# Queries and keys in one load, probabilities read back in four, output sums stored in one

## The chip, the cores and the metric

The kernel runs on one core of a Trainium2 chip. The metric is device time in microseconds, the median of several runs, as the host starts the program once and waits for its end. The core has five engines that run side by side: TensorE (PE, with its weight loads shown apart as PEld), VectorE (DVE), ScalarE (ACT), GpSimd (POOL) and SyncE (SP), which does no arithmetic and here issues nearly all DMA transfers. Each engine takes its instructions in order, and an instruction that has to wait for another engine or for a transfer holds up those behind it.

## The reference

Attention within chunks of 64 tokens, 8 batches of 8 heads, 576 tokens, 64 channels to a head; its rows, put together over the heads, go through a normalized, gated pair of layers:

```
scores = scale * q_c @ k_c.T          # per chunk of 64 tokens
attn   = softmax(scores)              # over the chunk
x      = (attn @ v_c)                 # 4608 rows of 8 * 64 = 512
xn     = x / sqrt(mean(x * x) + 1e-6) * rms_g
g, val = xn @ w_gate, xn @ w_val      # 512 -> 1536
out    = (g * sigmoid(g) * val) @ w_out   # 1536 -> 512
```

Everything is float32. The kernel splits each operand of the large products into a high and a low part and sums three matmuls.

## The kernel before

The attention is done in 18 units of 256 tokens (`UT`), each in two halves of 128 tokens, `i = 2 * u` and `2 * u + 1`. The layers are done in tiles of 512 tokens: three plain ones first (`t` = 0, 1, 2, the loop over `PLAIN`), then three pairs of tiles, in which the products are done by a Strassen-like scheme of seven products for eight on sums of blocks (`P1` to `P7`, the names of the products).

A unit goes through a list of steps, `unit_steps`, which are hung on the loop of the layers at numbered places (`PAIR_AT` and `PAIR_STEPS` and their like), so that its work lies between the large matmuls: `load_unit` loads queries and keys (L233, L234); `first` makes the scores on PE (L264) and the exponentials; `load_values` loads values (L240); `second` sums them and turns blocks of 32x32 on DVE (L355); `away` stores the probabilities of both halves to DRAM (L360, `away_e`); `third`, `turn_back`, reads them back in another arrangement (L371, tile `eT`); `fourth` multiplies them with the values (L388) and normalizes (L402 to L410, tile `xu`). In `mean_square` (L455) the tile `eT` serves as a place for squares nobody reads. Then `xu` is turned on DVE, stored (L421) and read back as `x` (L428). Units 0 to 3 use another way with transposes on PE (`att_transpose`, L321 to L323), which also writes a tile with the tag `eT`.

Before a tile can be written, the readers of what stood in its buffer must be done. The pool `io` has four buffers of 4 KB to a partition; queries `qt`, keys `kt`, values `vt`, `xu` and, during tile `t` = 1, the sums `w` of output weights take turns in them. The pool `att` has two buffers for `eT`.

Each unit's queries and keys are two transfers of 512 KB. The probabilities of a unit are read back in eight transfers of 64 KB, by half `s`, by `c` and by `k`, into two tiles, one for each `c`. The sums of output weights are made in `out_sides` in three steps: `sums` (L614 and L623 on DVE), `parts` (L627 on ACT, L628 on DVE), `store` (L633). There are 12 of them, four in tile `t` = 1 and eight in `t` = 2 (there in `spots` of the second `x` or in a tile of their own). Each is stored to the DRAM tensor `wol` in two transfers of two slots each. Beside them, in `t` = 1, `sides` loads converted weights back (L664), sums them on POOL (L659), splits them on ACT and DVE (L687, L689) and stores them (L688, L690). In the pairs the weights are read from DRAM by `ring_load` (L743, `wr`) and `out_load` (L859, L863, `wo`).

The order of the work: up to the end of `t` = 0 a planner that knows the durations of instructions only from a model orders all engines by priority; from `t` = 1 on PE keeps the order in which the program is written, and in the pairs SP, DVE and ACT keep it too. In `t` = 1 and 2 the planner still orders SP, DVE and ACT. By the profile `t` = 1 runs from about 150 to 254 us, `t` = 2 from there to 366, and the three pairs from there on.

Of the kernel before, what the change touches and what calls it, by code (L numbers as in the profile page):

```python
# [8 lines left out]
F32 = mybir.dt.float32  # L9
# [8 lines left out]
P = 128  # L18
CH = 64
D = 64  # L20
H = 8
NPAIR = H // 2
N = 4608
UT = 256
# [27 lines left out]
Q = 32  # L52
# [38 lines left out]
def tile_chunk_attn_swiglu(  # L91
    ctx: ExitStack,
    tc: tile.TileContext,
    qT: bass.AP,
    kT: bass.AP,
    v: bass.AP,
    w_up: bass.AP,
    w_out: bass.AP,
# [3 lines left out]
    nc = tc.nc  # L102
# [1 line left out]
    const = ctx.enter_context(tc.tile_pool(name="const", bufs=1))  # L104
    xs = ctx.enter_context(tc.tile_pool(name="xs", bufs=2 * NDT))
    dram = ctx.enter_context(tc.tile_pool(name="dram", bufs=1, space=bass.MemoryType.DRAM))
    io = ctx.enter_context(tc.tile_pool(name="io", bufs=4))
    wts = ctx.enter_context(tc.tile_pool(name="wts", bufs=3 * NF // 2))
    att = ctx.enter_context(tc.tile_pool(name="att", bufs=2))
    small = ctx.enter_context(tc.tile_pool(name="small", bufs=4))  # L110
# [28 lines left out]
    def bank(pool, name):  # L139
        return pool.tile([P, 512], F32, tag=pool_tag[id(pool)], name=name)  # L140
# [87 lines left out]
    state = {}  # L228

    def load_unit(u):  # L230
        qt = io.tile([P, NPAIR, UT], F32, tag="io", name="qt")
        kt = io.tile([P, NPAIR, UT], F32, tag="io", name="kt")
        nc.sync.dma_start(qt, qT[u])  # L233
        nc.sync.dma_start(kt, kT[u])  # L234
        for s in range(2):
            state[2 * u + s] = {"q": qt, "k": kt}

    def load_values(u):
        vt = io.tile([P, NPAIR, UT // CH, D], F32, tag="io", name="vt")
# [4 lines left out]
    def load_first_unit():  # L244

        qt, kt = (x[:, 2 * i : 2 * i + 2].rearrange("p s (a t) -> p (s a) t", t=UT) for i in range(2))
        for s in range(2):
            part = slice(s * P, (s + 1) * P)
            nc.sync.dma_start(qt[:, :, part], qT[0][:, :, part])
            nc.scalar.dma_start(kt[:, :, part], kT[0][:, :, part])  # L250
            state[s] = {"q": qt, "k": kt}

    def two_banks(pool, name):
# [62 lines left out]
    def att_transpose(i, pool=None):  # L316
        st = state[i]
        e = st["e"].rearrange("p a j k -> p a (j k)")
        eT = st["eT"] = att.tile([P, NPAIR, P], F32, tag="eT", name="eT")
        pt = bank(pool or ps_a, "ps_t").rearrange("p (a k) -> p a k", k=P)  # L320
        for pr in range(NPAIR):  # L321
            nc.tensor.transpose(pt[:, pr], e[:, pr], ident)
        nc.scalar.copy(eT, pt)  # L323
# [38 lines left out]
    def turn_back(i):  # L362
        st, s = state[i], i % 2
        if s == 0:
            state["eT", i // 2] = [att.tile([P, 2, H, Q], F32, tag="eT", name="eT") for _ in range(2)]
        eT, away = state["eT", i // 2], st["away"]
        back = away.rearrange("(c t p) (k r) -> c k p t r", c=2, t=2, k=2)
        for c in range(2):
            for k in range(2):
                dst = slice((2 * s + k) * Q, (2 * s + k + 1) * Q)  # L370
                nc.sync.dma_start(eT[c][dst].rearrange("p t h q -> p t (h q)"), back[c, k])  # L371

    def turned_values(u):
        subs = [state[2 * u + s] for s in range(2)]
        for st in subs:
            st["o"] = bank(ps_a, "ps_o")
        vt = subs[0]["v"].rearrange("p a n d -> p (a n d)").rearrange("p (c h d) -> p c h d", c=2, d=D)
        eT = state.pop(("eT", u))  # L380
        for s, st in enumerate(subs):
            st["eT"] = eT[s]
        for h in range(H):
            for t in range(2):
                for c in range(2):
                    for s, st in enumerate(subs):
                        rows = slice(s * CH, (s + 1) * CH)
                        nc.tensor.matmul(  # L388
                            st["o"][(2 * c + t) * Q : (2 * c + t + 1) * Q, h * D : (h + 1) * D],
                            eT[c][rows, t, h],  # L390
                            vt[rows, c, h],
                            start=True,
                            stop=True,
                        )
# [205 lines left out]
    def out_sides(i, c, home):  # L600

        cols = slice(c * P, (c + 1) * P)
        hi, lo = (
            out_parts[i][:, n].bitcast(F32).rearrange("p f (h c) -> p (f h) c", c=KH)[:, :, cols]
            for n in range(2)
        )
        slots = wol_.rearrange("p (k i) c -> p i k c", i=NPR)[:, i, :, c * KH : (c + 1) * KH]

        ws = []

        def sums():
            ws.append(home())
            w = ws[0]
            nc.vector.tensor_tensor(w[:, :, 0], hi, lo, op=ALU.add)  # L614
            a11, a21, a12, a22 = (w[:, n, 0] for n in range(4))
            s1, s2, s4, s3 = (w[:, n, 1] for n in range(4))
            for o, one, two, op in (
                (s1, a21, a22, ALU.add),
                (s2, s1, a11, ALU.subtract),
                (s4, a12, s2, ALU.subtract),  # L620
                (s3, a11, a21, ALU.subtract),
            ):
                nc.vector.tensor_tensor(o, one, two, op=op)  # L623

        def parts():
            w = ws[0]
            nc.scalar.copy(w[:, :, 0].bitcast(F32R), w[:, :, 1])  # L627
            nc.vector.tensor_tensor(w[:, :, 1].bitcast(F32R), w[:, :, 1], w[:, :, 0], op=ALU.subtract)  # L628

        def store():  # L630
            w = ws[0]
            for n in range(0, 4, 2):
                nc.sync.dma_start(slots[:, n : n + 2], w[:, n : n + 2].rearrange("p n a c -> p n (a c)"))  # L633

        return [sums, parts, store]

# [344 lines left out]
    def unit_steps(u, x):  # L981
# [19 lines left out]
        def third():  # L1001
            for i in both:
                turn_back(i)

        def fourth():
            turned_values(u)
            turned_norm(u)

        return [
            lambda: load_unit(u),  # L1010
            first,
            lambda: load_values(u),
# [9 lines left out]
    class Steps:  # L1022
# [4 lines left out]
        def __call__(self):  # L1027
            for f in self.at.get(self.n, ()):
                f()
            self.n += 1  # L1030

    load_first_unit()
    conv_load(0)
    load_values(0)
    load_unit(1)
    load_values(1)
    nc.sync.dma_start(g_col, rms_g)
# [5 lines left out]
    softmax(0)  # L1043
    softmax(1)
    att_transpose(0)
    softmax_sum(0)
    att_transpose(1)
    o = two_banks(ps_h, "ps_o")
    att_values(0, o)
# [6 lines left out]
    scores(3, s2)  # L1056
    softmax(3)
    att_transpose(2)
    softmax_sum(2)
    x_transpose_unit(0)  # L1060
# [11 lines left out]
    for t in range(PLAIN):  # L1072
        if t == 1:
# [3 lines left out]
            for n, u in enumerate((4, 5)):  # L1077
                for k, f in enumerate(unit_steps(u, x)):
                    at.setdefault(2 + 9 * n + FIRST_STEPS[k], []).append(f)
            at.setdefault(21, []).append(lambda: load_unit(2 * PLAIN))  # L1080
            half = Steps(at)
            for f, n in enumerate(OUT_FIRST):
# [3 lines left out]
            st = last.open("st", 1)  # L1086
# [6 lines left out]
        elif t == 2:  # L1093
            st = last.open("st2", 1)
# [8 lines left out]
            for n, (f, first) in enumerate(zip(range(len(OUT_FIRST), NF), OUT_AT)):  # L1103

                def home(n=n):
                    if n % 3 == 2 or n == 7:
                        return st.tile([P, 4, 2, P], F32, tag="t1", bufs=1, name="w")
                    return spots[n % 3]
# [10 lines left out]
        for f in range(NF):  # L1119
            g = gated(f, CONVS[f % 2], conv_step)  # L1120
            if t == 0:
                if f in (0, 5):
                    u = 2 + (f == 5)
# [40 lines left out]
    for b in range(NB):  # L1164
        t = PLAIN + 2 * b
# [5 lines left out]
        if not last_pair:  # L1171
            u = 2 * t + 4
# [94 lines left out]
```

## Time and profile before

| | us |
|---|---|
| median of three runs (lowest, highest) | 923.97 (921.32, 925.01) |
| the profiled execution | 921.97 |
| its span, from the first to the last instruction | 920.2 |

The profile is of one execution. Its span is cut into 40 slices, and each digit is the busy share of a slice in tenths, 9 being 90% or more; the row DMA is the mean busy share of the 16 DMA engines.

```profile
PE   5799999999999999999999999999999999999998
PEld 4578888887787878888787888787887888888886
DVE  6899986465687553876666997676668874344885
ACT  5988944353456564533344554344446632212452
POOL 0100012233300000122211000221220002211000
PEclk9999999999999999999999999999999999999999
DMA  9698999876997762487878975688688867335613
```

A group of instructions is named by its line in the kernel, its engine and what it writes and reads, as in "L388 PE ps_o<-vt,eT". Idle time of an engine is put down to what ended it, as in "<-DMA eT<-away_e": a transfer into `eT` from the stored probabilities. SPq stands for SP as it issues transfers; the duration there is that of the issue, not of the transfer.

### The profile page before, as it was taken

How to read it: one execution, taken by the hardware profiler on the slowest of the kernel's cores; microseconds unless marked ns; L12 is line 12 of the kernel's file. 1: busy time of each engine (PE TensorE's matmuls, PEld its weight loads, DVE VectorE, ACT ScalarE, POOL GpSimd, SP SyncE). 2: the span in 40 equal slices, each digit the busy share in tenths (PEclk: the TensorE clock that was granted, in tenths of full speed). 3: DMA queues.
4: the chain of work that ended last, by engine and by line, in shares of the span. 5: the costliest groups of instructions: out<-in, count | busy, mean ns of one | idle time of the engine just before them, and what ended most of it. 6: DMA issues, size and time to landing. Idle time of an engine off the chain costs nothing.

```text
span 920.2 us, 17319 instructions
## 1 busy us (share of the span) xinstructions
PE 886.1 (96%) x6828; PEld 723.0 (79%) x6828; DVE 642.3 (70%) x1071; ACT 445.0 (48%) x731; POOL 128.3 (14%) x141
## 2 busy tenths in 40 slices
PE   5799999999999999999999999999999999999998
PEld 4578888887787878888787888787887888888886
DVE  6899986465687553876666997676668874344885
ACT  5988944353456564533344554344446632212452
POOL 0100012233300000122211000221220002211000
PEclk9999999999999999999999999999999999999999
DMA  9698999876997762487878975688688867335613
GB/s 353 274 331 304 365 322 343 293 255 205 289 333 240 221 184 88 183 299 256 313 250 256 324 274 205 219 300 315 226 301 271 311 249 302 138 142 193 238 60 124
DMA packets 97649, 233.40 MB, mean 254 GB/s; under 512 B 8864, under 2 KB 60576, under 8 KB 84896
## 3 DMA queue, kind: packets, MB, share of 16 engines
q1 hardware_dynamic: 96512, 231.77, 71.5%
q8 instruction: 54, 0.88, 0.4%
q10 hardware_dynamic: 1056, 0.52, 0.2%
q14 instruction: 27, 0.22, 0.1%
HBM read 167.25 MB, written 65.01 MB: 252 GB/s over the span
## 4 chain that ended last, share of the span: by engine, by line
PE 76%; DVE 7%; DMA 5%; ACT 5%; POOL 2%; issue 2%; SPq 1%; DVEq 0%; ACTq 0%; POOLq 0%
PE ps_b L751 10%; PE ps_a L751 10%; PE ps_c L751 10%; PE ps_g L545 6%; PE acc L580 6%; PE ps_v L545 6%; PE ps_d L751 5%; PE ps_a L926 5%; PE ps_b L926 5%; PE ps_c L926 5%; PE ps_d L926 3%; PE ps_s L264 2%; POOL w L659 1%; PE ps_o L388 1%; DMA away_x<-xu 1%
## 5 line engine op out<-in xcount | busy, mean ns | idle before, releaser
L751 PE MATMUL ps_b<-xp,wr 128*128 128x512 f32 x432 | 106.2, 396 | 3.0 <-DVE rs L347 1.9
L849 DVE TENSOR_TENSOR gl<-g,gh 128x512 fp32r<-128x512 f32 x126 | 85.7, 688 | 28.3 <-ACT gh L848 27.3
L848 ACT CAST gh<-g 128x512 fp32r<-128x512 f32 x126 | 73.1, 619 | 65.5 <-PE ps_b L926 20.6
L751 PE MATMUL ps_c<-xp,wr 128*128 128x512 f32 x432 | 104.6, 391 | 0.0
L751 PE MATMUL ps_a<-xp,wr 128*128 128x512 f32 x432 | 103.5, 390 | 0.0
L545 PE MATMUL ps_g<-xh,parts 128*128 128x512 f32 x288 | 97.7, 398 | 3.1 <-ACT sg L563 2.9
L751 PEld LDWEIGHTS ps_b<-xp,wr 128*128 128x128 f32 x432 | 81.6, 190 | 21.0 <-DVE rs L347 2.3
L545 PE MATMUL ps_v<-xh,parts 128*128 128x512 f32 x288 | 95.6, 392 | 0.0
L751 PEld LDWEIGHTS ps_a<-xp,wr 128*128 128x128 f32 x432 | 80.9, 188 | 16.9
L751 PEld LDWEIGHTS ps_c<-xp,wr 128*128 128x128 f32 x432 | 80.6, 188 | 17.1
L580 PE MATMUL acc<-parts,gh 128*128 128x512 f32 x288 | 90.2, 394 | 1.4 <-ACT gh L568 1.4
L815 POOL TENSOR_TENSOR g<-c,c 128x512 f32<-128x512 f32 x18 | 23.3, 1293 | 323.5 <-DVE c L811 223.2
L545 PEld LDWEIGHTS ps_g<-xh,parts 128*128 128x128 f32 x288 | 54.7, 190 | 16.2 <-ACT sg L563 4.0
L545 PEld LDWEIGHTS ps_v<-xh,parts 128*128 128x128 f32 x288 | 54.4, 189 | 11.8 <-DVE sg L567 0.4
L580 PEld LDWEIGHTS acc<-parts,gh 128*128 128x128 f32 x288 | 53.1, 188 | 13.0 <-ACT gh L568 1.9
L545 PE MATMUL ps_g<-xl,parts 128*128 128x512 f32 x144 | 56.7, 394 | 0.0
L545 PE MATMUL ps_v<-xl,parts 128*128 128x512 f32 x144 | 56.3, 391 | 0.0
L580 PE MATMUL acc<-parts,gl 128*128 128x512 f32 x144 | 56.3, 391 | 0.0
L751 PE MATMUL ps_d<-xp,wr 128*128 128x512 f32 x216 | 52.0, 390 | 0.5 <-DMA wr<-wsd 0.5
L926 PE MATMUL ps_c<-gh,wo 128*128 128x512 f32 x144 | 45.8, 392 | 2.2 <-DVE xu L402 1.9
L751 PEld LDWEIGHTS ps_d<-xp,wr 128*128 128x128 f32 x216 | 40.4, 188 | 9.3 <-issue 0.9
L567 DVE TENSOR_TENSOR sg<-ps_v,sg 128x512 f32<-128x512 f32 x36 | 24.6, 683 | 30.7 <-PE ps_v L545 26.5
(143 smaller groups left out, 1641.1 us busy)
## 6 DMA issues: line engine op xcount, KB each, us to landing
wr<-wsd SPq DMA_DIRECT2D x63, 1024.0 KB, 7.5
raw<-w_up_dram SPq DMA_DIRECT2D x12, 1024.0 KB, 7.9
wo<-wol SPq DMA_DIRECT2D x12, 1024.0 KB, 6.9
vt<-v_dram SPq DMA_DIRECT2D x18, 512.0 KB, 6.5
wsd<-parts SPq DMA_DIRECT2D x18, 512.0 KB, 7.4
wo<-wod SPq DMA_DIRECT2D x9, 1024.0 KB, 8.8
qt<-qT_dram SPq DMA_DIRECT2D x17, 512.0 KB, 6.3
kt<-kT_dram SPq DMA_DIRECT2D x17, 512.0 KB, 6.4
```

What stands on the lines that cost most here:

```text
L264: nc.tensor.matmul(st["s"][j][c * CH : (c + 1) * CH, pr], st["q"][rows, pr, tok : tok + CH], st["k"][rows, pr, tok : tok + CH], start=True ...
L388: nc.tensor.matmul(st["o"][(2 * c + t) * Q : (2 * c + t + 1) * Q, h * D : (h + 1) * D], eT[c][rows, t, h], vt[rows, c, h], start=True, sto ...
L545: nc.tensor.matmul(ps, a[f][:, cols], b[dt], start=(dt == 0 and i == 0), stop=(dt == NDT - 1 and i == 2),)
L567: nc.vector.tensor_tensor(sg, pv, sg, op=ALU.mult)
L580: nc.tensor.matmul(acc[s], a[:, cols], b, start=(f == 0 and i == 0), stop=(f == NF - 1 and i == 2),)
L659: nc.gpsimd.tensor_tensor(out, one, two, op=op)
L751: nc.tensor.matmul(ps, w[:, a, m, cols], xp[:, b, kt], start=start and kt == 0 and i == 0, stop=stop and kt == 1 and i == 2, skip_group_ch ...
L815: nc.gpsimd.tensor_tensor(g[:, 1, 1], kp["c22"], kept[0]["c22"], op=mult)
L848: nc.scalar.copy(gh, src)
L849: nc.vector.tensor_tensor(gl, src, gh.bitcast(F32), op=ALU.subtract)
L926: nc.tensor.matmul(ps[m][INTO[p]], w[:, m, a], parts[c], start=p in FROM and i == 0 and j == 0, stop=p in LAST and i == NPR - 1 and j == 2 ...
```

## The change

Queries and keys are put together on the host into one array, with both next to each other for each partition, and one transfer of 1 MB brings both into a tile of 8 KB to a partition that has one buffer. The first unit, which is loaded in parts, reads from the same array. `io` keeps two buffers for values, `xu` and `w`. The two tiles of a unit's probabilities become one of 4 KB to a partition with one buffer, read back in one transfer for each half `s` and each `k`, 128 KB each; in units 0 to 3 both halves share such a tile too. A sum of output weights is stored in one transfer of 512 KB.

```diff
@@ tile_chunk_attn_swiglu
-    io = ctx.enter_context(tc.tile_pool(name="io", bufs=4))
+    io = ctx.enter_context(tc.tile_pool(name="io", bufs=2))
...
@@ load_unit
-        qt = io.tile([P, NPAIR, UT], F32, tag="io", name="qt")
-        kt = io.tile([P, NPAIR, UT], F32, tag="io", name="kt")
-        nc.sync.dma_start(qt, qT[u])
-        nc.sync.dma_start(kt, kT[u])
+        t = io.tile([P, 2, NPAIR, UT], F32, tag="qk", bufs=1, name="qk")
+        nc.sync.dma_start(t, qk[u])
         for s in range(2):
-            state[2 * u + s] = {"q": qt, "k": kt}
+            state[2 * u + s] = {"q": t[:, 0], "k": t[:, 1]}
...
@@ load_first_unit
-            nc.sync.dma_start(qt[:, :, part], qT[0][:, :, part])
-            nc.scalar.dma_start(kt[:, :, part], kT[0][:, :, part])
+            nc.sync.dma_start(qt[:, :, part], qk[0][:, 0, :, part])
+            nc.scalar.dma_start(kt[:, :, part], qk[0][:, 1, :, part])
...
@@ att_transpose
-        eT = st["eT"] = att.tile([P, NPAIR, P], F32, tag="eT", name="eT")
+        if i % 2 == 0:
+            state["eT", i // 2] = att.tile([P, 2, NPAIR, P], F32, tag="eT", bufs=1, name="eT")
+        eT = st["eT"] = state["eT", i // 2][:, i % 2]
...
@@ turn_back
-            state["eT", i // 2] = [att.tile([P, 2, H, Q], F32, tag="eT", name="eT") for _ in range(2)]
+            state["eT", i // 2] = att.tile([P, 2, 2, H, Q], F32, tag="eT", bufs=1, name="eT")
         eT, away = state["eT", i // 2], st["away"]
-        back = away.rearrange("(c t p) (k r) -> c k p t r", c=2, t=2, k=2)
-        for c in range(2):
-            for k in range(2):
-                dst = slice((2 * s + k) * Q, (2 * s + k + 1) * Q)
-                nc.sync.dma_start(eT[c][dst].rearrange("p t h q -> p t (h q)"), back[c, k])
+        back = away.rearrange("(c p) (k r) -> k p c r", c=4, k=2)
+        for k in range(2):
+            dst = eT[(2 * s + k) * Q : (2 * s + k + 1) * Q]
+            nc.sync.dma_start(dst.rearrange("p c t h q -> p (c t) (h q)"), back[k])
...
@@ turned_values
-            st["eT"] = eT[s]
+            st["eT"] = eT[:, s]
...
-                            eT[c][rows, t, h],
+                            eT[rows, c, t, h],
...
@@ out_sides, store
-            for n in range(0, 4, 2):
-                nc.sync.dma_start(slots[:, n : n + 2], w[:, n : n + 2].rearrange("p n a c -> p n (a c)"))
+            nc.sync.dma_start(slots, w.rearrange("p n a c -> p n (a c)"))
...
@@ kernel, on the host
-        "qT": heads_first(q),
-        "kT": heads_first(k),
+        "qk": np.stack([heads_first(q), heads_first(k)], axis=2),
```

More of the change, by code (lines that the diff above doesn't have):

```diff
@@ L93, in tile_chunk_attn_swiglu @@
     tc: tile.TileContext,
-    qT: bass.AP,
-    kT: bass.AP,
+    qk: bass.AP,
     v: bass.AP,
```

## The prediction

> **What bounds the kernel now.** The first view is the page's head and its table of busy time; the second is the table of busy time in stretches that I chose at the kernel's stages. In a row of that table the columns after the stretch are its length and the busy time of PE, PEld, DVE, ACT and POOL with instruction counts, then the granted clock, the DMA share and GB/s.
>
> ```profile
> span 920.2 us, 17319 instructions
> PE 886.1 (96%) x6828; PEld 723.0 (79%) x6828; DVE 642.3 (70%) x1071; ACT 445.0 (48%) x731; POOL 128.3 (14%) x141
> ...
> 0.00:64.00 64.00, 46.93 (x465) 36.95 (x466) 51.50 (x93) 49.10 (x93) 4.57 (x11) 1.00 0.84 318
> 64.00:200.00 136.00, 136.00 (x1022) 111.41 (x1021) 103.29 (x156) 85.47 (x146) 22.75 (x18) 1.00 0.89 315
> 200.00:254.00 54.00, 50.68 (x342) 40.92 (x341) 33.81 (x53) 24.70 (x41) 18.58 (x16) 1.00 0.82 257
> 254.00:366.00 112.00, 108.05 (x1187) 87.55 (x1186) 69.95 (x156) 60.58 (x90) 7.40 (x16) 1.00 0.66 216
> 366.00:690.00 324.00, 318.55 (x2826) 260.27 (x2825) 235.00 (x395) 142.19 (x228) 53.49 (x62) 0.99 0.75 264
> 690.00:920.00 230.00, 225.89 (x994) 185.90 (x992) 148.79 (x222) 82.99 (x137) 21.47 (x19) 1.00 0.56 203
> ```
>
> The reader is to see that TensorE sets the time: 886.1 us of 920.2. Length minus PE busy gives its idle time by stage: 17.1 us in the first 64, none from 64 to 200, 3.3 from 200 to 254, 4.0 from 254 to 366, 5.5 in the stretch of the pairs up to 690, 4.1 after it. The clock is 0.99 or 1.00 all the way, so nothing is to be had there. The change alters no matmul; it can only win from those idle times or add to them. The third view says what ended them: who waited for whom, for PE (in total, times, longest).
>
> ```profile
> PE ps_g L545 <- ACT sg L563: 2.9, 2, 1.9
> PE ps_s L264 <- DMA kt<-kT_dram: 2.1, 2, 1.7
> PE ps_c L926 <- DVE xu L402: 1.9, 1, 1.9
> ...
> PE acc L580 <- ACT gh L568: 1.4, 1, 1.4
> ...
> PE ps_o L388 <- DMA eT<-away_e: 1.0, 1, 1.0
> ...
> PE ps_d L751 <- DMA wr<-wsd: 0.5, 1, 0.5
> ```
>
> The transfers that the change touches are named for 2.1 us (keys) and 1.0 us (probabilities read back), and one transfer behind them on SP for 0.5 us. The wait of 1.9 us for `xu` hangs on DVE's own fixed order (L402 behind additions) and stays.
>
> **The change part by part.** The columns here are instructions, KB of one, and median us from issue to landing.
>
> ```profile
> wr<-wsd SPq DMA_DIRECT2D x63, 1024.0 KB, 7.5
> ...
> qt<-qT_dram SPq DMA_DIRECT2D x17, 512.0 KB, 6.3
> ...
> eT<-away_e SPq DMA_DIRECT2D x112, 64.0 KB, 4.3
> ...
> wol<-w SPq DMA_DIRECT2D x14, 256.0 KB, 3.5
> ```
>
> Instructions removed from SP: 17 of the 34 loads of queries and keys (the keys' 17 are like the queries' in the row), 56 of the 112 reads of probabilities, and 12 of the 24 stores of sums (14 from `w` above, 10 more from `x`). No byte is removed, and the runs of bytes of the reads and stores stay 1 KB. What one costs SP is the first column of durations here (min/median/max, ns), and the eight in a row below show what they cost together:
>
> ```profile
> L233 SPq DMA_DIRECT2D qt<-qT_dram x17: 383/441/1119, 3.5 to 633.7; - x17
> L371 SPq DMA_DIRECT2D eT<-away_e x112: 302/426/1924, 171.3 to 678.3; - x112
> L633 SPq DMA_DIRECT2D wol<-w x14: 370/456/817, 136.0 to 332.1; - x14
> ...
> 395.27 7.52 SPq L371 DMA_DIRECT2D eT<-away_e  x8
> ...
> SPq L371 <- DMA wr<-wsd: 19.6, 7, 3.4
> ```
>
> By medians that is 17 x 0.44 + 56 x 0.43 + 12 x 0.46 = 37 us of SP's time. Hardly any of it lies on the path that sets the end: SP issues ahead of TensorE, and from 366 on PE lost 0.5 us to a transfer. The batch of eight even takes 7.52 us there, twice 8 x 0.43, because seven such reads waited 19.6 us in all for a weight transfer issued earlier; with four reads most of that goes, and the weights behind (L743) leave up to 5.8 us sooner (7.52 - 4 x 0.43). What is late next is DVE, not they.
>
> [...]
>
> So the gain is worked out at the three places where PE waited. The fourth wait, 0.4 us in the first stage, goes from the keys' 2.1 minus the 1.66 below; the same megabyte lies behind the same earlier loads there, so I take 0 (between 0 and 0.4).
>
> ```profile
> 289.69 0.39 SPq L233 DMA_DIRECT2D qt<-qT_dram  x1
> 293.14 0.32 SPq L421 DMA_DIRECT2D away_x<-xu  x1
> 293.58 0.36 SPq L234 DMA_DIRECT2D kt<-kT_dram  x1
> ...
> 298.18 0.63 PE L264 MATMUL ps_s<-kt,qt 64*64 64x64 f32 x27 [1.66 <-DMA kt<-kT_dram]
> ...
> 333.52 1.74 SPq L371 DMA_DIRECT2D eT<-away_e  x4
> 338.06 0.34 SPq L421 DMA_DIRECT2D away_x<-xu  x1
> 338.45 1.77 SPq L371 DMA_DIRECT2D eT<-away_e  x3
> 340.95 1.73 SPq L428 DMA_DIRECT2D x<-away_x  x4
> 342.71 0.43 SPq L371 DMA_DIRECT2D eT<-away_e  x1
> ...
> 345.70 0.48 PE L388 MATMUL ps_o<-vt,eT 64*32 64x64 f32 x33 [0.97 <-DMA eT<-away_e]
> ```
>
> First the keys, at 298.18. The keys stood on SP behind the store of `xu`, which waited for DVE; the queries had left 3.9 us before. One transfer goes out as one. Where the queries stood it lands, as an estimate from the 7.5 us of the 1 MB row, at 297.2, and PE, ready at 298.18 - 1.66 = 296.52, waits 0.7: a gain of 1.0. Issued earlier still, it gains 1.66. Where the keys stood, it lands at 301.1 by the same row: a loss of 2.9. Its buffer comes free with the scores of the unit before, so I take the early place and 1.3.
>
> Then the probabilities, at 345.70. The eighth read left 4.3 us behind the start of the three before it (342.71 - 338.45), after four reads of `x`. With four, two leave at 333.5 and two by 339: the wait of 0.97 goes whole (between 0 and 0.97; I take 1.0). Last the weights, 0.5 us: two or three issues fewer are ahead of that load; I take 0.4 (between 0 and 0.5). Together -2.7.
>
> The rest of the change moves buffers. The pool `io` falls from four buffers to two, for values, `xu` and the `w` of the output sums; queries and keys get one of 8 KB, probabilities one of 4 KB. In the pairs each unit uses four `io` tiles and had four, so each role there already waited for the unit before; the values now wait for the products of the previous values, as the keys' buffer did, and `wr` behind them is held no longer than before. Cost 0; without that cover it is the one 0.5 us wait again. In the stage from 150 to 254 it is different, because there `w` shares the pool:
>
> ```profile
> 186.82 0.33 SPq L240 DMA_DIRECT2D vt<-v_dram  x1
> ...
> 200.87 0.45 SPq L421 DMA_DIRECT2D away_x<-xu  x1
> ...
> 201.12 0.68 DVE L614 TENSOR_TENSOR w<-parts 128x512 f32<-128x512 f32 x1
> 204.45 0.68 DVE L614 TENSOR_TENSOR w<-parts 128x512 f32<-128x512 f32 x1
> ...
> 225.73 0.90 SPq L633 DMA_DIRECT2D wol<-w  x2
> 229.26 3.52 DVE L689 TENSOR_TENSOR w<-w,side 128x512 fp32r<-128x512 f32 x3 [6.70 <-ACT side L687]
> ...
> L623 DVE TENSOR_TENSOR w<-w x28: 232/283/1373, 132.4 to 320.1; 128x128 f32<-128x128 f32 x28
> ```
>
> At 201 to 205 two `w` are made while the values of 186.82 and the `xu` that leaves at 200.87 still hold buffers: four live tiles. With two, the first `w` waits for `xu` to land, and the second for the first to be stored, past 225.73 in the old order. Each is two operations of 128x512, 0.68 us, and four of 0.28 on DVE. Behind a waiting one on DVE stand the operations of the gate (L567), for which ACT and then PE wait. The price is between 0 (the planner puts it into the 6.70 us in which DVE was idle) and, as an estimate, 6.0 us: 2.5 us of operations (2 x 0.68 + 4 x 0.28) and the 3.5 us in which such a store lands. I take 0.7, near the low end, because those 6.70 us lie where the buffer comes free.
>
> Sum: -2.7 + 0.7 = -2.0 us. The profiled execution took 921.97 us, its span 920.2 and 1.8 around it; it would take 919.97. It stands 2.0 under the median of the runs, 923.97; on that median the forecast is **922.0**.
>
> **The rivals.** The first: nothing moves (924.0). The bytes are the same, PE is busy 96%, and where a wait goes, DVE or ACT, which feed the next matmul, may set the same start. For it: no stall at all from 64 to 200, where as many transfers are issued. Against it: the two places shown, where SP's order alone made the transfer late. [...]
>
> The second is slower, from the two buffers. DVE stands at the deferred `w` in the stage of 200 to 254, and TensorE with it. It costs all 6.0 us, and no gain is set against it: 930.0. It decides from the point where DVE reaches the deferred sums before the store has landed, with a gate queued behind them. For it: the rows above, and the gate waits of 2.9 and 1.4 us, which show that PE has no slack left around there. Against it: before 366 the planner orders DVE itself and can place the sums later.
>
> The third is faster, by a freed SP. In the stages from 200 to 366 SP issues side weights, loads for POOL and reads of probabilities in one line, and the gate waits (2.9 and 1.4) come after such chains. If the shorter line loosens all of them, the 3.3 us and the 4.0 us of idle time go, and the 0.5: 7.8 us, 916.2. Against it: much of that idle time ends on ACT and DVE, which keep all their work.
>
> That the change doesn't do what it says would show in the counts of issues; I give it no chance of its own.
>
> **How the numbers follow.** The forecast of -2.0 has 0.42, its own range 920.4 (the gains whole, 1.66 + 0.97 + 0.5 + 0.4 = 3.5) to 924; nothing moves 0.18; slower 0.20; faster 0.20. A measurement of this kernel can tell about 0.5%, 4.6 us, from no change: the bounds are 919.4 and 928.6. The first two cases lie within, 0.60; the slower case is past the upper one, 0.20, the faster past the lower, 0.20. The range of 8 in 10 reaches to the worked-out time of each outer case, rounded outward, 916.0 to 930.0, leaving out about half of each. Another order of the first 64 us, which the planner makes too, isn't worked out; small shifts of it lie inside the range.
>
> **What would show it.** Right: 17, 56 and 12 issues; no PE wait for keys over 1 us after 100 us, none for probabilities; batches of four that take about 2 us; idle time of 254 to 366 near 2 us and of 200 to 254 at most 4. Wrong: a wait of DVE at L614 for a store or of PE at the gate, idle time of 200 to 254 above 6 us; a load of queries and keys issued where the keys stood; the first 64 us longer or shorter by over 2 us, which no step here foresees.

## The result and the profile after

Seven runs of the changed kernel have a median of 917.75 us (915.42 to 919.90), seven of the kernel before beside them 923.97 (920.35 to 925.01). The ratio on record is 0.9942, with a 95% interval from 0.9924 to 0.9960: 5.4 us faster (3.7 to 7.0); the two medians alone would give 0.9933. The forecast was 922.0, 2.0 us faster, in a range from 916 to 930. So the time fell in the range, but the case "within 0.5%", which had 0.60, didn't come; "faster by over 0.5%", which had 0.20, did, by a little. The profiled execution took 918.96 us, 3.0 less than that of before, and a second pair of profiles 917.83 against 922.96, 5.1 less.

First the page's head and the table of busy time by stage for the changed kernel, with the columns and the stretches of before; then who waited for whom, for PE, of which three rows from behind 64 us are shown.

```profile
span 916.8 us, 17164 instructions
...
0.00:64.00 64.00, 47.10 (x468) 37.00 (x469) 52.11 (x93) 49.53 (x93) 4.57 (x11) 1.00 0.86 320
64.00:200.00 136.00, 135.48 (x1020) 111.16 (x1019) 104.99 (x159) 85.68 (x147) 23.00 (x18) 1.00 0.90 316
200.00:254.00 54.00, 50.66 (x339) 40.22 (x338) 32.93 (x51) 23.73 (x39) 18.71 (x16) 1.00 0.78 248
254.00:366.00 112.00, 108.35 (x1188) 87.35 (x1188) 70.31 (x156) 63.67 (x93) 7.42 (x16) 1.00 0.67 217
366.00:690.00 324.00, 320.84 (x2839) 261.40 (x2838) 235.74 (x398) 145.12 (x234) 54.26 (x64) 1.00 0.79 265
...
PE acc L578 <- ACT gh L566: 2.0, 1, 2.0
...
PE ps_o L386 <- DMA eT<-away_e: 1.7, 2, 1.5
...
PE ps_d L748 <- DMA wr<-wsd: 1.1, 1, 1.1
```

The reader is to see that little moved up to 366 us: idle time there was 17.1, 0, 3.3 and 4.0 us, and is 16.9, 0.5, 3.3 and 3.7. In the stretch of the pairs it fell from 5.5 us to 3.2. The two waits of 1.9 us "for DVE" are gone (`xu`, which the prediction left standing, and `rs`, which it didn't name), though the change removes nothing from DVE. The counts of issues are as said: `qk` 17, `eT` 56, `wol` 12.

Since the stages shift against each other, the table that the rest of this text uses takes the length of stages from PE's instructions in order of time: tiles 1 and 2 from the first transpose of `x` for tile 1 to the first product of pair 1; pair 1 and pair 2 each from the first product to the first of the next pair. What lies ahead of tile 1 (137.4 to 138.6 us) and pair 3 (171.5 us in every run) hardly differ. A stage is from one execution; the ratio is from 6 to 12 runs against the kernel before.

| kernel | ratio to before, 95% | tiles 1, 2 | pair 1 | pair 2 |
|---|---|---|---|---|
| before; again | | 230.7; 231.8 | 189.3; 188.8 | 186.5; 187.1 |
| changed; again | 0.9942 (0.9924 to 0.9960) | 231.1; 231.1 | 186.1; 185.4 | 186.0; 186.0 |
| e1 before, four reads | 0.9959 (0.9937 to 0.9982) | 229.9 | 185.3 | 186.4 |
| e2 before, one load | 0.9962 (0.9933 to 0.9991) | 227.7 | 191.9 | 185.1 |
| e3 before, one store | 1.0017 (0.9994 to 1.0040) | 231.3 | 185.6 | 186.5 |
| e4 before, weights earlier | 0.9962 (0.9937 to 0.9987) | 230.6 | 187.2 | 184.5 |
| a1 changed, eight reads | 0.9946 (0.9925 to 0.9966) | 226.1 | 191.1 | 186.0 |
| a2 changed, weights earlier | 0.9917 (0.9886 to 0.9948) | 227.7 | 184.5 | 184.6 |
| a3 changed, spare issues | 0.9986 (0.9964 to 1.0008) | 230.6 | 187.3 | 187.4 |
| a4 changed, loads split | 0.9932 (0.9914 to 0.9951) | 226.1 | 186.6 | 188.7 |
| b1 before, buffers only | 0.9946 (0.9921 to 0.9970) | 227.1 | 190.2 | 185.0 |
| a5 a4 and weights earlier | 0.9924 (0.9895 to 0.9952) | 228.9 | 185.0 | 185.6 |

Two things have to be kept in mind with it. The ratio of the changed kernel is from a session in which the kernel before had a median of 923.97 us; beside the other rows it had 921.1 to 921.4. By medians alone the changed kernel (917.75) lies beside e1, e2, e4, a1 and b1 (916.8 to 917.7), a4 2.0 and a2 3.5 us under it, and a3 only 1.3 us over it. And the stages of the pairs hold a second kind of stall, which the profile names "issue" and to which the last section comes back: in pair 1 it is 3.3 us in a1, 3.2 in e2, 2.8 in b1, 2.5 in e4, 1.6 in the second profile of before, 1.2 in the first of the changed kernel and 0 in the first of before. Less this stall, pair 1 takes 187.2 to 189.3 us in the kernels with eight reads and weights loaded as before (e3, with 184.8, is the exception), and 183.6 to 186.1 in those with four.

### The profile page after: what moved, and what is told of

It is laid out like the page before. It is cut to its first block, busy times and chain, and to the rows that moved or that the text cites. A ratio compares the mean times of both kernels' runs of the same rounds, so it can differ in the third digit from the quotient of the medians.

```text
span 916.8 us, 17164 instructions
## 1 busy us (share of the span) xinstructions
PE 885.4 (97%) x6828; PEld 721.2 (79%) x6828; DVE 643.9 (70%) x1071; ACT 447.7 (49%) x733; POOL 128.6 (14%) x141
## 4 chain that ended last, share of the span: by engine, by line
PE 71%; ACT 7%; issue 7%; DVE 7%; DMA 5%; POOL 3%; SPq 1%; ACTq 0%; DVEq 0%; POOLq 0%
PE ps_c L748 11%; PE ps_a L748 10%; PE ps_b L748 10%; PE ps_a L923 5%; PE ps_d L748 5%; PE ps_b L923 5%; PE ps_v L543 5%; PE ps_g L543 4%; PE acc L578 4%; PE ps_c L923 4%; PE ps_d L923 3%; PE ps_s L261 2%; POOL w L656 1%; DMA away_x<-xu 1%; PE ps_o L386 1%
## 5 line engine op out<-in xcount | busy, mean ns | idle before, releaser
L923 PE MATMUL ps_a<-gh,wo 128*128 128x512 f32 x144 | 45.3, 389 | 0.0
```

The source lines that it names most:

```text
L923: nc.tensor.matmul(ps[m][INTO[p]], w[:, m, a], parts[c], start=p in FROM and i == 0 and j == 0, stop=p in LAST and i == NPR - 1 and j == 2 ...
```

## The experiments

**Which part brings the gain.** The theory after the result: in the pairs PE waited for weights that left SP late, behind the eight reads, and the profile put it down to DVE. The rival: another part, above all the merged load, brings the gain. Three kernels do one part each.

e1, the kernel before with the new `turn_back` (and `att_transpose`, `turned_values` to match):

```diff
-        for c in range(2):
-            for k in range(2):
-                dst = slice((2 * s + k) * Q, (2 * s + k + 1) * Q)
-                nc.sync.dma_start(eT[c][dst].rearrange("p t h q -> p t (h q)"), back[c, k])
+        for k in range(2):
+            dst = eT[(2 * s + k) * Q : (2 * s + k + 1) * Q]
+            nc.sync.dma_start(dst.rearrange("p c t h q -> p (c t) (h q)"), back[k])
```

> The kernel before with only the probabilities read back in four transfers (tile of both blocks, one buffer). Theory: in the pairs, eight reads in a row hold SP until an earlier weight transfer has landed, and the weights behind leave too late; so the four PE stalls of before in the pairs (1.90 at 442, 1.92 at 501, 0.47 at 593, 1.06 at 631, 5.35 us in all) shrink to under 3 us, and the time falls by 2 to 4 us (ratio 0.996 to 0.998). Rival (the merged load of queries and keys brings it): ratio 1.000, the stalls as before.

Measured 0.9959: 3.8 us faster, as the theory said; PE's waits named for weights in the pairs sum to 0.5 us. In its profile pair 1 is 4.0 us shorter than before, the other stages under 1 us. e2, the kernel before with the merged load and its buffers:

```diff
-        qt = io.tile([P, NPAIR, UT], F32, tag="io", name="qt")
-        kt = io.tile([P, NPAIR, UT], F32, tag="io", name="kt")
...
+        t = io.tile([P, 2, NPAIR, UT], F32, tag="qk", bufs=1, name="qk")
+        nc.sync.dma_start(t, qk[u])
```

> The kernel before with only queries and keys in one transfer (one buffer of 8 KB, io of two buffers). Theory: ratio 0.998 to 1.000; the wait for keys near 298 us (1.66) goes, the stalls in the pairs stay at 4 us or more, as eight reads still follow one weight transfer. Rival (this load brings the gain): ratio 0.994 to 0.996, stalls in the pairs under 3 us.

Measured 0.9962, 3.5 us faster, more than the theory gave it. The gain lies elsewhere: tiles 1 and 2 take 227.7 us, 3 less, and pair 1 takes 191.9, no less than before (3.2 us of it at "issue"). e3, with the store alone:

```diff
-            for n in range(0, 4, 2):
-                nc.sync.dma_start(slots[:, n : n + 2], w[:, n : n + 2].rearrange("p n a c -> p n (a c)"))
+            nc.sync.dma_start(slots, w.rearrange("p n a c -> p n (a c)"))
```

> The kernel before with only the sums of output weights stored in one transfer. Both theories: ratio 0.999 to 1.001, since these stores lie between 135 and 332 us and PE waited for none; the stalls in the pairs as before (4 to 6 us). A ratio under 0.997 would speak for a third one, that the shorter line of SP in the stages up to 366 us brings the gain.

Measured 1.0017: the stores bring nothing, as expected. Its one profile shows pair 1 at 185.6 us with eight reads, though, as short as with four, with 1.5 us of waits for weights in the pairs where 4 to 6 us of stalls were expected, while its runs are not faster. So the stall in pair 1 isn't the same in every execution, and a stage of one profile is to be read with some 3 us of doubt; the ratios decide.

**Whether the waits of before were for weights.** e4 leaves the kernel before as it is and loads weights one transfer further ahead:

```diff
-AHEAD_R = 3
-AHEAD_O = 3
+AHEAD_R = 4
+AHEAD_O = 4
```

> The kernel before with weights loaded one transfer further ahead (AHEAD_R and AHEAD_O 4 instead of 3), nothing else. Theory (PE's stalls in the pairs are late weights, though the profile names DVE): the stalls at 442, 501, 593 and 631 go, 5.35 us to under 1.5, ratio 0.994 to 0.996, without any part of the change. Rival, as the prediction had it (they belong to DVE's order): stalls stay, ratio 1.000.

Measured 0.9962, 3.5 us: just outside the expected 0.994 to 0.996, which its interval covers. This is PE's wait list of e4 from 366 to 700 us, whole:

```profile
PE ps_o L388 <- issue: 2.5, 1, 2.5
PE ps_c L926 <- ACT gh L848: 0.5, 2, 0.2
PE ps_c L926 <- DVE gl L849: 0.5, 2, 0.2
```

None of the four waits of before is left, neither the one named for a transfer nor the three named for DVE. DVE's instructions and their order in the pairs are those of before. What is new, 2.5 us at "issue", is taken up below. The kernel before itself says the same when its rows are put beside the transfers. First SP in order of time around three of the waits, with the start, the duration of the issue and the count; then PE's three instructions, with what ended the idle time before them; then the time from issue to landing of the first `wr` at 434.85, of the first `wo` at 495.02 and of the first `wr` at 623.97.

```profile
422.43 0.33 SPq L421 DMA_DIRECT2D away_x<-xu  x1
422.81 0.42 SPq L743 DMA_DIRECT2D wr<-wsd  x1
423.28 9.36 SPq L371 DMA_DIRECT2D eT<-away_e  x8
432.69 2.12 SPq L428 DMA_DIRECT2D x<-away_x  x4
434.85 1.38 SPq L743 DMA_DIRECT2D wr<-wsd  x3
...
485.00 7.25 SPq L371 DMA_DIRECT2D eT<-away_e  x8
...
495.02 0.91 SPq L863 DMA_DIRECT2D wo<-wol  x2
...
623.97 1.39 SPq L743 DMA_DIRECT2D wr<-wsd  x3
...
441.97 0.79 PE L751 MATMUL ps_b<-xp,wr 128*128 128x512 f32 x2 [1.90 <-DVE rs L347]
501.09 0.47 PE L926 MATMUL ps_c<-gh,wo 128*128 128x512 f32 x1 [1.92 <-DVE xu L402]
631.17 1.17 PE L751 MATMUL ps_b<-xp,wr 128*128 128x512 f32 x4 [1.06 <-DVE e L355]
...
DMA to landing us min/median/max: 7.0/7.0/7.0
DMA to landing us min/median/max: 5.9/5.9/5.9
DMA to landing us min/median/max: 7.1/7.1/7.1
```

434.85 + 7.0 = 441.85, and PE starts at 441.97; 495.02 + 5.9 = 500.92, and PE starts at 501.09; 623.97 + 7.1 = 631.07, and PE starts at 631.17. By the packed trace each of the three instructions waits for the semaphore of just that load (109, 101 and 101), beside one of DVE (106) and, at 501.09, one of ACT (108). At the first place the weights that PE needs had left 12.4 us behind the store of `xu` (422.43), since the batch of eight held SP for 9.36 us. In the second profile of the kernel before the first two of these instructions carry the right name:

> The kernel before once more, for a second profile. If the weight stalls of the first profile are the kernel's own: pair 1 (its seven products and the way back, from the first product to the end) near 189 us and 3 to 6 us of weight stalls in the pairs; the two tiles ahead of the pairs near 231 us. If they are a matter of one execution: pair 1 near 185.5 and stalls under 2 us, as in the run with the store alone.

```profile
443.17 0.70 PE L751 MATMUL ps_b<-xp,wr 128*128 128x512 f32 x2 [1.51 <-DMA wr<-wsd]
500.93 0.47 PE L926 MATMUL ps_c<-gh,wo 128*128 128x512 f32 x1 [0.62 <-DMA wo<-wol]
```

Pair 1 took 188.8 us there, 1.6 of it at "issue". The waits at the same four places sum to 4.2 us, two of them again named for DVE, and two more for weights elsewhere add 0.9: they come again in a second execution, though e3 shows that they can also be small with eight reads. The same places in the changed kernel:

```profile
423.25 0.42 SPq L740 DMA_DIRECT2D wr<-wsd  x1
423.76 3.96 SPq L369 DMA_DIRECT2D eT<-away_e  x4
427.83 6.78 SPq L426 DMA_DIRECT2D x<-away_x  x4
434.73 1.30 SPq L740 DMA_DIRECT2D wr<-wsd  x3
...
482.83 2.53 SPq L369 DMA_DIRECT2D eT<-away_e  x4
485.46 3.92 SPq L426 DMA_DIRECT2D x<-away_x  x4
489.72 0.94 SPq L860 DMA_DIRECT2D wo<-wol  x2
...
SPq L426 <- DMA wr<-wsd: 11.3, 4, 4.0
```

Four reads take 4.0 and 2.5 us instead of 9.36 and 7.25, but part of it comes back a line later: the four reads of `x` (L426) now wait for the earlier weights, 11.3 us from 366 to 690 where the eight reads of `eT` waited 17.8. Near 490 us the weights leave some 5 us sooner. Near 434 they leave at the same time as before, and the wait of 1.90 went because they landed 5.1 us after their issue instead of 7.0; why they landed sooner stays open. In the second profiles they left at 432.31 there instead of 435.92.

**Whether it is the number of transfers.** a1 puts eight reads of 64 KB back into the changed kernel (the diff of e1, reversed), and a3 adds four spare transfers of 1 KB to the four reads:

```diff
             nc.sync.dma_start(dst.rearrange("p c t h q -> p (c t) (h q)"), back[k])
+            spare = att.tile([16, 16], F32, tag="spare", bufs=8, name="spare")
+            nc.sync.dma_start(spare, v[0][:16, 0, 0, :16])
```

> The changed kernel with the probabilities read back in eight transfers again. Theory (late weights behind the reads): weights are late in the pairs again, 2 to 5 us of PE stalls, ratio to before 0.996 to 0.999, 2 to 4 us over the changed kernel. Rival (the merged load alone brings it): ratio 0.993 to 0.996.

> The changed kernel with four spare transfers of 1 KB added to a unit's four reads, one behind each; nothing reads them. Theory (the number of transfers holds SP, by its issue time and by the wait for an earlier transfer): the batch takes 6 us or more where a weight transfer stands ahead of it, SP waits there for that transfer again, ratio to before 0.997 to 1.000. Rival (the size of the reads brings the gain): ratio as the changed kernel, 0.993 to 0.995.

a3 gave back nearly all by the ratios: 0.9986. SP in a3, where a weight transfer stands ahead of the batch, and behind the dots PE's waits from 254 to 366 us:

```profile
393.31 0.42 SPq L742 DMA_DIRECT2D wr<-wsd  x1
393.82 0.38 SPq L369 DMA_DIRECT2D eT<-away_e  x1
394.25 0.47 SPq L371 DMA_DIRECT2D spare<-v_dram  x1
394.78 0.47 SPq L369 DMA_DIRECT2D eT<-away_e  x1
395.29 0.50 SPq L371 DMA_DIRECT2D spare<-v_dram  x1
395.83 0.44 SPq L369 DMA_DIRECT2D eT<-away_e  x1
396.31 0.44 SPq L371 DMA_DIRECT2D spare<-v_dram  x1
398.63 0.30 SPq L369 DMA_DIRECT2D eT<-away_e  x1
401.99 0.33 SPq L371 DMA_DIRECT2D spare<-v_dram  x1
...
PE ps_o L388 <- DMA eT<-away_e: 3.8, 2, 3.1
```

The eighth transfer behind the weights of 393.31, a mere 1 KB, left 8.7 us after them, which is about the time such weights take to land (median 8.4 in the changed kernel). It is the same place in the row at which the last of the eight reads of before (432.34) and the last of the four reads of `x` after the change (434.30) were held. So here it is the number of transfers that holds SP, not their bytes. The packed trace of the kernel before also tells why it is the eighth: SP's transfers use eight semaphores in turn (67 to 69 uses of each) for their landing, and none of the 538 transfers for which an earlier one had used the semaphore left before that one had landed. The last read left at 432.34 and has a wait for semaphore 101 in the trace; the weights of 422.81, eight transfers ahead of it, have the same semaphore and landed at 432.33. In the changed kernel the read of 434.30 shares semaphore 107 with the weights of 423.25, which landed at 434.29. In both the hold is thus a wait for a landing, which the program contains.

What the four transfers cost in time is less clear. By the ratios a3 lies 4 us over the changed kernel, by the medians 1.3. PE waited 3.8 us in tile 2 for late reads of probabilities, yet tiles 1 and 2 are no longer than in the changed kernel; the two pairs are 2.6 to 3.3 us longer together, and the larger part of that are stalls at "issue" (3.0 us against 1.2 and 0.5).

a1 missed its theory's ratio: 0.9946, no worse than the changed kernel. The table and PE's waits in the pairs show why. The waits for weights are back, 4.1 us (`wr` 2.0, `wo` 2.1), as the theory says; 2.3 of them lie in pair 1. Pair 1 took 191.1 us, 5 more, but 3.3 of that are the stall at "issue", which the theory knows nothing of. And tiles 1 and 2 took 226.1, 5 less. There is a second effect, in tiles 1 and 2.

**The second effect, and the merged load.** a4 splits the load in the changed kernel again, into the same tile; b1 gives the kernel before only new buffers, with its two loads and eight reads (the first part of the diff is a4's, the other two are b1's):

```diff
-        nc.sync.dma_start(t, qk[u])
+        for n in range(2):
+            nc.sync.dma_start(t[:, n], qk[u][:, n])
...
-    io = ctx.enter_context(tc.tile_pool(name="io", bufs=4))
+    io = ctx.enter_context(tc.tile_pool(name="io", bufs=2))
...
-        qt = io.tile([P, NPAIR, UT], F32, tag="io", name="qt")
-        kt = io.tile([P, NPAIR, UT], F32, tag="io", name="kt")
+        qt = io.tile([P, NPAIR, UT], F32, tag="qt", bufs=1, name="qt")
+        kt = io.tile([P, NPAIR, UT], F32, tag="kt", bufs=1, name="kt")
```

> The changed kernel with queries and keys in two transfers again, into the same tile with its own buffer. If the merged load's share of the gain is the number of transfers: ratio to before 0.996 to 0.998, 1.5 to 3 us over the changed kernel. If it is the buffer of its own, from which both leave early: ratio as the changed kernel, 0.993 to 0.995.

> The kernel before with only the buffers of the loads changed: queries and keys one buffer each of their own, io two buffers, and two transfers of 512 KB as before. Theory (the load's share of the gain comes from its buffers, since splitting it again lost nothing): ratio 0.994 to 0.997, the two tiles ahead of the pairs 226 to 228 us, no wait for keys near 298. Rival (the merged transfer): ratio 1.000, 230 to 231 us.

a4 has 0.9932 and b1 0.9946. So the load's share comes from the buffers, and that the transfer is one adds nothing that these runs can tell. With buffers of their own, queries and keys no longer wait for a value's or an `xu`'s buffer. In b1 they leave at 279.98 and 280.66 instead of 289.69 and 293.58, tiles 1 and 2 take 227.1 us, and the wait for keys near 298 is gone. The changed kernel has these buffers and yet 231.1 us there, in both profiles:

> The changed kernel once more, for a second profile. Theory: pair 1 near 186 us, weight stalls in the pairs under 2 us. The two tiles ahead of the pairs took 231.1 us in the first profile but 226.1 with the loads split: if the first was one slow execution, 226 to 228 now; if the merged load costs it, 231 again.

Pair 1 took 185.4 us, as expected, but the waits for weights in the pairs sum to 2.5 us, more than the expected 2. Tiles 1 and 2 took 231.1 again. The merged load alone doesn't cost that: e2, which has it with the same buffers, took 227.7. These are PE's three largest waits from 254 to 366 us in the changed kernel, and then, behind the dots, in a1, which has the same buffers for the loads and took 226.1, its only one:

```profile
PE ps_o L386 <- DMA eT<-away_e: 1.7, 2, 1.5
PE ps_g L543 <- ACT sg L561: 0.7, 1, 0.7
PE ps_o L386 <- PE ps_v L543: 0.7, 1, 0.7
...
PE ps_o L385 <- DMA eT<-away_e: 0.8, 1, 0.8
```

The keys' wait (1.66 before) went and the others came or stayed; all waits of this stretch sum to 3.6 us against 0.8 in a1, which is 2.8 of the 5 us. In these tiles the planner orders SP, DVE and ACT, and it makes another order for each combination of parts. That this order costs the buffers' gain in the changed kernel, and not with the load split (a4) or weights further ahead (a2), is the likely reading; it is argued, not shown. Which instruction in the order costs it was not isolated and stays open.

**A better version.** a2 is the changed kernel, a5 is a4, each with weights one transfer further ahead (the diff of e4).

> The changed kernel with weights loaded one transfer further ahead (AHEAD_R and AHEAD_O 4). Theory: the change and this remedy remove the same stalls, so the gains don't add up: no weight stall in the pairs, ratio to before 0.992 to 0.995, no more than 2 us under the changed kernel. Rival (the change's gain has another source): the gains add, 0.988 to 0.991.

> The changed kernel with queries and keys in two transfers into its tile, and weights one transfer further ahead (AHEAD_R and AHEAD_O 4). Theory: no weight stall in the pairs, the two tiles ahead near 226 us: ratio to before 0.990 to 0.992, as good as or better than the changed kernel with weights earlier (0.9917). Rival (the fetch stalls of PE inside the pairs take it back): 0.993 to 0.995.

a2 has 0.9917, a median of 914.22 us, and no wait for weights in the pairs: pair 1 and pair 2 take 184.5 and 184.6 us, the least of all. That is 7.6 us under the kernel before (4.8 to 10.5), though its interval overlaps that of the changed kernel, 0.9942. a5, at 0.9924 and with 228.9 us in tiles 1 and 2 where 226 was expected, adds nothing to it. a2's ratio lies between what its theory (0.992 to 0.995) and its rival (0.988 to 0.991) gave. By the profiles the two pairs are 2.3 to 3.0 us shorter than in the changed kernel, so the gains of the four reads and of earlier weights overlap in part, and tiles 1 and 2 are 3.4 us shorter, at 227.7.

## Why the prediction was right in its range and too small in its gain

- *The number.* The time fell in the range, but not by the sum, and so by luck: of its 2.7 us of gains 2.3 (keys and probabilities) didn't come, and the gain came from a term that stood at 0.4.
- *The bound.* Right: PE sets the time. Between the first two profiles its idle time fell from 34.1 to 31.4 us and its busy time by 0.7.
- *The clock.* "0.99 or 1.00 all the way" holds by stage and hides one place. In the kernel before the granted clock is 0.57 on average from 442 to 446 us, behind the wait at 442; in the changed kernel it is 1.00 there. By the packed trace it is 0.5 for 3.4 us from 442.44, which is worth some 1.7 us on top of the wait (an estimate, half of 3.4): the twelve products there took 4.58 us, and twelve of `ps_a` from 448.26 took 3.02. The products behind the stall at "issue" in pair 1 of e2, b1 and a1 are about as slow, 4.44 and 4.45 us for twelve and 4.28 for eleven; behind the shorter stall in the second profile of before, of 1.6 us, twelve took 3.01.
- *Waits in the pairs.* This step failed. The prediction read "ps_c <- DVE xu 1.9" as DVE's own order, that "stays"; it saw that weights would leave up to 5.8 us sooner and said that "What is late next is DVE, not they", with 0.4 us for the one wait named for `wr`. In fact all three waits named for DVE end where a weight transfer lands, and the fourth, at 593, was named for one. Their going was worth 3.2 to 3.4 us in pair 1 (189.3 and 188.8 against 186.1 and 185.4, with 1.6 us at "issue" in 188.8 and 1.2 in 186.1), and 0.5 to 1.1 in pair 2. The trace held the means to see it: each of these waits ends within 0.2 us of the landing of a load that SP had issued late.
- *Keys, 1.3 us.* The wait went, as the early place was right: `qk` left at 278.91, long ahead of the 289.69 of the queries. But the stage didn't get shorter (231.1 against 230.7 and 231.8), since other waits took its place: gain 0, and the forecast counted on 1.3.
- *Probabilities, 1.0 us.* Wrong: 1.7 us of waits are left (1.1 in the second profile), and the batches of four took 4.0 and 2.5 us where 2 was foretold. The planner again put the last read behind the four reads of `x`, at 342.72 against 342.71 before.
- *The sums' `w` in two buffers, +0.7.* The mechanism was right and the price near 0:

```profile
205.78 0.71 DVE L612 TENSOR_TENSOR w<-parts 128x512 f32<-128x512 f32 x1 [3.88 <-DMA away_x<-xu]
...
233.07 0.68 DVE L612 TENSOR_TENSOR w<-parts 128x512 f32<-128x512 f32 x1
```

  The first `w` waited 3.88 us for `xu` to land; the second moved from 204 to 233, past the store. The gate waited 1.3 us near 212, as I read it for this `w`, in place of a wait of 1.9 near 214; idle time from 200 to 254 is 3.3 us as before. So the slower rival didn't come, for the reason given against it.
- *The faster rival* had the right engine, a freed SP, and the wrong place: not the gates from 200 to 366, whose idle time is as before, but the weights in the pairs.
- *SP's issue time.* Hardly any of the 37 us, the prediction said, lies on the path that sets the end. For the merged load and the merged store the runs agree: split again, the load lost nothing (a4, 0.9932 beside 0.9942), and the store brought nothing (e3, 1.0017). For the reads they differ from it: the eighth transfer behind a weight transfer is held until that one has landed (432.34 behind 432.33), and so what stands behind the reads leaves late.

The medians differ by more than the first two profiles do, 6.2 us against 3.0. The spans of the second pair differ by 5.5, of which pair 1 has 3.4, pair 2 1.1, and tiles 1 and 2 and what lies ahead 1.1; that is as far as single executions go.

## What to carry to other kernels

Where a wait is named for an engine, put its end beside the landing times of the transfers that the waiting instruction reads; the last to land can be the cause (here of waits of 1.90, 1.92 and 1.06 us), and what SP had to issue ahead of it is the place to work on. Loading further ahead is the cheap test of it and here the better remedy (no wait for weights was left in the pairs in e4 and a2, while e1 had 0.5 us). And where a planner orders part of the kernel, a part that gains alone may gain nothing beside another, so each combination has to be measured.

## What the runs showed of the hardware

Fewer transfers were not sooner ones here: the 128 KB reads of `eT` in the changed kernel land 6.4 us after their issue (median; 4.3 for the 64 KB of before), and the reads of `x`, which are as before, 5.9 instead of 3.1.

In several runs PE stood still amid the 128 small matmuls of `turned_values`, with nothing that it waited for; here e2:

```profile
446.79 0.31 PE L385 MATMUL ps_o<-vt,eT 64*32 64x64 f32 x5 [3.23 <-issue]
```

It was 3.3 us in a1, 2.5 in e4, 1.6 in the second profile of before, and 0 in a2; in four runs it stands at the products just behind (1.2 us in the changed kernel). The profile pages of the kernel before, the changed kernel, e2 and a2 each count 54 packets, 0.88 MB, on queue q8 of the kind "instruction", 16 KB each. The packed traces have the times of these packets: in all runs together there are 16 stalls named "issue" behind 64 us, and each ends 1.2 to 1.5 us after such a packet has landed; the one shown ends at 446.79, and a packet landed at 445.50; that of the changed kernel ends at 446.78, and a packet landed at 445.44. That PE's instructions come late there at times, for which the expectation of a5 has the name fetch stalls, is a reading of these times that no run tested. Why the stalls lie at these places, and why in some executions only, was not tested either.
